# A SwiGLU down projection in seven products of halves, on a TensorE-bound kernel

## The chip, the cores and the metric

One core of one Trainium2 chip. The metric is the device time of one execution in microseconds (us). A core has these engines, each with its own queue, which it works through in the order of the program: TensorE (PE; loads of its stationary operand are shown as PEld), VectorE (DVE), ScalarE (ACT), GpSimd (POOL) and SyncE (SP), which here issues most of the DMAs. Matrix products go to PSUM, which PE writes and DVE and ACT read; everything else lies in SBUF.

## What is computed

A normalised input goes into two branches: attention over the last 512 positions of a cache (32 heads of 192), and a SwiGLU feed-forward network. The Silu of the second gates the first.

```
x  = A_x                                   # 2048 x 640
xn = layernorm(x)
s  = attention(xn, k_cache, v_cache, wq, wo)
h  = silu(xn @ w_gate) * (xn @ w_up)       # 2048 x 1536
g  = silu(h @ w_down)                      # w_down: 1536 x 640
out = x + s * g
```

The change concerns `h @ w_down` and the Silu around it.

## The kernel before

The kernel has three stages. The first, up to 171 us of the profiled execution, is the feed-forward network with the layer norm in front of it. The second, by far the longest, runs attention over 16 pairs of heads. The third is the output projection. Both attention's query projection and the output projection already use fewer products than a plain matrix product would: they add halves of operands first (`combine_wq`, `combine_x`, `a_sum`, `wo_sums`) and add halves of results later.

**The feed-forward stage.** The 2048 rows form four blocks of 512 (`b`), the 1536 hidden columns 12 groups of 128 (`f`). The loop from line 488 runs over `b` and, in it, over `f`. One step does:

- `ffn_hidden(b, f)` (line 377): ten products of 128x128 by 128x512 into a PSUM tile `sc` of two banks, five for the gate half, five for the up half; ACT takes the Silu of one half (line 374), and DVE multiplies it with the other into `hTs[b][:, f, :]` (line 375), which holds the hidden values transposed: 128 hidden columns on the partitions, 512 rows. There are two `sc` tiles in turn, so the products of step `f + 2` need the multiply of step `f`. Block 0 has its first four groups before the loop.
- `wo_sums` (line 346), in two of every three steps: DVE adds pieces of the output projection's weights, two sums in the first of the three steps, three in the second, into a tile `wo_s` that exists once; after the fifth sum SP stores it to `wo_d` (line 360), so the next group of sums, two steps on, waits until this store has landed. `wo_pieces` loads the pieces two groups ahead.
- in blocks 0 to 2, `ln_stats` (DVE, steps 2 to 5) and `ln_apply` with a DMA transpose (steps 6 and 7) for the next block's rows, whose loads SP issues at step 0.
- in blocks 2 and 3, one entry of `xwork` per step: a sum over blocks of `xn` (`combine_x`, DVE, 0.67 to 0.95 us each), which attention's query projection needs later. In the same blocks, the first pair's keys are loaded, transposed, summed and centred, and its query weights laid out.
- in blocks 1 to 3, at steps 1, 4, 7 and 10, `ffn_down(b - 1, u)` (line 383): one tile of 128 rows of the block before. For each of 12 hidden groups it runs two products of 128x128 by 128x320, into the two banks of one `mm` tile; then one ACT Silu over both halves (line 393) and one SP store of 128x640 to `g_d` (line 394).

After the loop (line 549) the last block's four `ffn_down` follow, with six `q_full` (line 396: five products of 128x512 and an ACT copy) between them, which project the first queries. There are two `mm` tiles in turn, used by `ffn_down`, `q_full` and, later, attention. Attention starts with `scores_phase(0, 0)`, in which `q_rows` writes `mm` tiles and `scores` writes `sc` tiles.

Buffers that attention uses later and that are empty in most of the feed-forward stage: `m_f` (32-bit sums of queries), the second buffer of each of `wq_p`, `khat` and `qT`.

All instructions stand in each engine's queue in the order in which the Python program issues them (`manual_schedule`); waits between engines are put in by the framework.

Of the kernel before, what the change touches and what calls it, by code (L numbers as in the profile page):

```python
# [9 lines left out]
ACT = mybir.ActivationFunctionType  # L10
ALU = mybir.AluOpType
# [4 lines left out]
def kernel(  # L16
# [13 lines left out]
    nc = tc.nc  # L30
    P = nc.NUM_PARTITIONS
# [3 lines left out]
    Sq, D = x2.shape  # L35
    _, Hkv, Sk, Dh = A_k_cache.shape
# [3 lines left out]
    W = min(4096, max(256, Sk // 4))  # L40
    assert Dh == 192 and W == 512 and Hkv == H and H % 2 == 0
    assert D % P == 0 and F % P == 0 and Sq % 512 == 0
    NC = D // P
    T = Sq // P
    NB = Sq // 512
    KC = W // P
    NF = F // P
# [4 lines left out]
    HC = D // 2  # L52
# [3 lines left out]
    bf = dt.bfloat16  # L56
    h16 = dt.float16
    f32 = dt.float32
# [10 lines left out]
    kpool = ctx.enter_context(tc.tile_pool(name="att_k", bufs=1))  # L69
    qpool = ctx.enter_context(tc.tile_pool(name="att_q", bufs=2))  # L70
# [3 lines left out]
    wpool = actx.enter_context(tc.tile_pool(name="att_w", bufs=2))  # L74
# [5 lines left out]
    def sc_tile():  # L80
        return sc_pool.tile([P, 2, 512], f32, name="sc")

    def mm_tile(which=None):
        which = mm_next[0] if which is None else which
        mm_next[0] = 1 - which
        return mm_pool[0].tile([P, 2, 512], f32, name="mm", tag="mm%d" % which)
# [8 lines left out]
    m_f = res.tile([P, 2, 2, 512], f32, name="m_f")  # L95

    o_d = dram.tile([T, P, 2 * KH, P], bf, name="o_d")
    g_d = dram.tile([T, P, D], bf, name="g_d")
# [110 lines left out]
    def q_of(i, j):  # L209
        return q_pair(i)[:, 3 * (i % 2) + j, :]  # L210
# [15 lines left out]
    with ExitStack() as fctx:  # L226
# [4 lines left out]
        ffa = fctx.enter_context(tc.tile_pool(name="ffa", bufs=3, side="right"))  # L231
# [5 lines left out]
        wd_sb = ffw.tile([P, NF, D], bf, name="wd_sb")  # L237
# [3 lines left out]
        def load_x(t, engs=(nc.sync,)):  # L241
            x_t[t] = lnx.tile([P, D], bf, name="x_t")
            n = P // len(engs)
            for k, eng in enumerate(engs):
                r = slice(k * n, (k + 1) * n)
                eng.dma_start(out=x_t[t][r, :], in_=x2[t * P + r.start : t * P + r.stop, :])
# [24 lines left out]
        for t in range(4, 8):  # L271
# [9 lines left out]
        first = [  # L281
            [gu[:, s, :] for s in range(2)]
            for gu in (sc_tile(), sc_tile(), psum1.tile([P, 2, 512], f32, name="gu"))
        ]
# [21 lines left out]
        def ln_rstd(b, t0, t1):  # L306

            mv, rstd = ln[b]
            nc.gpsimd.tensor_scalar(rstd[:, t0:t1], mv[:, t0:t1, 1], EPS, None, op0=ALU.add)
            nc.gpsimd.tensor_tensor(rstd[:, t0:t1], rstd[:, t0:t1], nhalf[:, t0:t1], ALU.pow)  # L310
# [24 lines left out]
        hTs, won = {}, {}  # L335
# [10 lines left out]
        def wo_sums(n, ks):  # L346

            t = won[n]
            if not ks.start:
                won["sums"] = ffw.tile([P, len(B_SUMS), 2, HC], h16, name="wo_s")  # L350
            sums = won["sums"]

            def piece(q):
                return t[:, q[0], :, q[1] * HC : (q[1] + 1) * HC]

            for k in ks:
                x, y, op = B_OF[B_SUMS[k]]
                nc.vector.tensor_tensor(sums[:, k, :, :], piece(x), piece(y), op)
            if ks.stop == len(B_SUMS):
                nc.sync.dma_start(  # L360
                    out=wo_d[:, :, 2 * n : 2 * n + 2, :].rearrange("s p c d -> p s c d"), in_=sums[:, :, :, :]
                )
# [9 lines left out]
        def hidden_gate(b, f, g, u):  # L372
            sg = ffa.tile([P, 512], bf, name="sg")
            nc.scalar.activation(sg[:], g, ACT.Silu)  # L374
            nc.vector.tensor_tensor(hTs[b][:, f, :], u, sg[:], ALU.mult)  # L375

        def ffn_hidden(b, f, gu=None):
            gu = gu or [sc[:, s, :] for sc in (sc_tile(),) for s in range(2)]
            for s in range(2):
                hidden_mm(gu[s], s, f, slice(b * 512, (b + 1) * 512))  # L380
            hidden_gate(b, f, *gu)

        def ffn_down(b, u):

            dn, rows = mm_tile(), slice(u * P, (u + 1) * P)
            for f in range(NF):
                for n in range(2):
                    nc.tensor.matmul(  # L388
                        dn[:, n, 0:HC], hTs[b][:, f, rows], wd_sb[:, f, n * HC : (n + 1) * HC],
                        start=(f == 0), stop=(f == NF - 1),  # L390
                    )
            g_t = ffa.tile([P, D], bf, name="g_t", bufs=2)
            nc.scalar.activation(g_t[:].rearrange("p (n d) -> p n d", n=2), dn[:, :, 0:HC], ACT.Silu)
            nc.sync.dma_start(out=g_d[4 * b + u, :, :], in_=g_t[:])

        def q_full(i, j):
            pr, b = divmod(i, NB)
            q_ps = mm_tile()[:, 0, :]
            for c in range(NC):
                nc.tensor.matmul(  # L400
                    q_ps[:, :], pairs[pr]["wq"][:, AS_IS[j], c, :], xnT[:, c, b * 512 : (b + 1) * 512],
                    start=(c == 0), stop=(c == NC - 1),
                )
            nc.scalar.copy(q_of(i, j), q_ps[:, :])
# [54 lines left out]
        for t in range(4):  # L459
            rows = slice(t * P, (t + 1) * P)  # L460
# [25 lines left out]
        xwork = []  # L486

        for b in range(NB):
            if b:
                hTs[b] = ffh.tile([P, NF, 512], bf, name="hT")  # L490
            nx = b + 1 < NB
            u = 0
            for f in range(NF):
                if nx and b and f == 0:
                    for t in range(4 * b + 4, 4 * b + 8):
                        load_x(t)
                if b or f >= 4:
                    ffn_hidden(b, f)
                n, phase = divmod((b - 1) * NF + f, 3)
                if n < KH // 2 and (b or n >= -2):  # L500
                    if b and phase < 2:
                        wo_sums(n, (range(0, 2), range(2, len(B_SUMS)))[phase])
                    if phase == 1 and n + 2 < KH // 2:
                        wo_pieces(n + 2)
                if nx and 2 <= f < 6:
                    ln_stats(4 * b + 2 + f)
                    if f == 5:
                        ln_rstd(b + 1, 0, 4)
                if nx and f in (6, 7):
                    for t in range(4 * b + 2 * f - 8, 4 * b + 2 * f - 6):  # L510
                        ln_apply(t)
                        ln_transpose_dma(t)
                if b == 2 and f == 0:
                    for half in range(2):
                        swap_x(DIFF[0], half, half)
                elif b == 2 and f == 8:
                    swap_x(DIAG, 0, 0)
                    xwork += x_combinations(DIFF[0]) + x_combinations(SUM[0])
                elif b == 3 and f == 0:
                    for half in range(2):  # L520
                        swap_x(DIFF[1], half, 2 + half)
                    swap_x(DIAG, 1, 3)
                elif b == 3 and f == 2:
                    xwork += [
                        u for to in (SUM[1], DIFF[1], DIAG) for u in x_combinations(to)
                    ]
                if xwork:
                    xwork.pop(0)()

                if b >= 1 and f in (1, 4, 7, 10):  # L530
                    ffn_down(b - 1, u)
                    u += 1
                if b == 2:
                    if f == 0:
                        load_k(0)
                    elif f == 3:
                        transpose_k(0)
                    elif f == 6:
                        load_wq(0)
                    elif 7 <= f < 10:  # L540
                        sum_k(0, f - 7)
                    elif f == 11:
                        combine_wq(0)
                elif b == 3:
                    if f < 5:
                        centre_k(0, f)
                    elif f < 7:
                        (load_k, load_wq)[f - 5](1)
        early_q = [(i, j) for i in range(2) for j in range(3)]
        for u in range(4):  # L550
            ffn_down(NB - 1, u)
            for _ in range((0, 2, 2, 2)[u]):
                q_full(*early_q.pop(0))
            if xwork:
                xwork.pop(0)()
        nc.scalar.activation(act_t[:], one_t[:], ACT.Exp)

# [247 lines left out]
    def store(n, side, cols=slice(0, D), eng=nc.sync):  # L805
        r = ROW_PAIRS[n][side]
        eng.dma_start(out=out2[r * P : (r + 1) * P, cols], in_=xg[n, side][:, 0, cols])

    V = nc.vector
# [8 lines left out]
    def total(to, x, y, op=ALU.add):  # L818
        V.tensor_tensor(to, x, y, op)
# [221 lines left out]
```

## Time and profile before

| what | value |
|---|---|
| median of three runs | 896.6 us (896.43 to 898.16) |
| the profiled execution | 898.59 us, span of its instructions 896.8 us |
| mean granted clock of TensorE | 0.996 |
| PE busy from 60 to 160 us, and from 160 to 180 us | 100.00 of 100 us, 19.54 of 20 us |
| `ffn_down`: products | 384 of 128x320, in 16 tiles, first 39.1 us, last 168.8 us |
| `ffn_down`: Silu | 16 of 128x640, mean 704 ns |
| `ffn_down`: stores | 16 of 160 KB, 1.8 to 6.2 us to landing, median 4.7 us |
| load of `w_down` | issued at 12.9 us, 12.7 us to landing |
| store of the wo sums | 12 of 800 KB, median 4.8 us to landing |

A time of an operation runs from its start to its end, and on DVE and PE the next one starts somewhat earlier than that end. Products on PE are pipelined: one of 320 columns has a length of 299 ns, but the next one starts long before. The chain of waits shows such a row of products with the time it holds PE. "Idle" at the end of a line is the time that the engine stood still in front of it, with what ended the wait.

### The profile page before, as it was taken

What the parts mean: (1) busy time and instruction counts of PE and PEld (TensorE: products, weight loads), DVE (VectorE), ACT (ScalarE), POOL (GpSimd) and SP (SyncE); (2) the same over time, 40 slices, a digit from 0 to 9 for tenths busy, and PEclk for the clock granted to TensorE, in tenths of its full rate; (3) what the DMA queues carried; (4) which work ended last, traced back from release to release, by engine and by line L of the source; (5) the groups of instructions that cost most, each with busy time, mean ns of one, the idle gap of its engine ahead of it and who ended that gap; (6) DMA issues with size and microseconds to landing.
All of it is one profiled execution on the core that took longest, in us unless ns stands there. A gap on an engine that the chain in (4) does not pass through costs nothing.

```text
span 896.8 us, 22912 instructions
## 1 busy us (share of the span) xinstructions
PE 879.9 (98%) x9705; PEld 582.5 (65%) x9705; DVE 599.0 (67%) x1020; ACT 404.2 (45%) x577; POOL 114.2 (13%) x215
## 2 busy tenths in 40 slices
PE   9999999999999999999999999999999989999997
PEld 6455555567667666667667666666676756777775
DVE  6464775276776776877777776777775367666664
ACT  4222222565765765765765765766757200000000
POOL 0000001012222222122212222222200000000000
PEclk9999999999999999999999999999999999999999
DMA  9669876256986979886986976978889997655520
GB/s 300 168 190 260 225 221 198 60 99 155 238 180 147 175 193 199 167 170 150 241 176 149 171 184 122 212 177 171 177 205 234 253 342 247 204 182 173 177 72 15
DMA packets 270822, 165.50 MB, mean 185 GB/s; under 512 B 173952, under 2 KB 265984, under 8 KB 270080
## 3 DMA queue, kind: packets, MB, share of 16 engines
q1 hardware_dynamic: 262896, 149.99, 69.9%
q10 hardware_dynamic: 7824, 14.06, 4.6%
q8 instruction: 76, 1.25, 0.6%
q14 instruction: 26, 0.21, 0.1%
HBM read 88.18 MB, written 40.24 MB: 143 GB/s over the span
## 4 chain that ended last, share of the span: by engine, by line
PE 90%; DMA 6%; DVE 2%; SPq 1%; issue 1%; ACTq 0%; ACT 0%
PE sc L645 18%; PE acc L780 15%; PE mm L591 12%; PE sc L367 11%; PE mm L684 10%; PE sc L684 9%; PE mm L577 8%; PE mm L388 6%; DMA b_w<-in_A_wo_dram 3%; DMA V_p<-in_A_v_cache_dram 2%; PE mm L400 1%; SPq L716 1%; DVE a_s L773 1%; DMA x_t<-in_A_x_dram 1%; PE gu L367 0%
## 5 line engine op out<-in xcount | busy, mean ns | idle before, releaser
L649 ACT ACTIVATE p_t<-sc 128x1024 bf16<-128x1024 f32 x256 | 253.7, 1024 | 60.0 <-PE sc L645 55.5
L645 PE MATMUL sc<-qT,khat 64*128 64x512 bf16 x1536 | 198.0, 376 | 0.0
L684 PEld LDWEIGHTS <-p_t 64*128 64x128 bf16 x4096 | 172.9, 94 | 14.3 <-DMA V_p<-in_A_v_cache_dram 4.1
L645 PEld LDWEIGHTS <-khat 64*128 64x128 bf16 x1536 | 89.0, 94 | 75.1 <-issue 0.3
L780 PEld LDWEIGHTS <-a_s 128*128 128x128 f16 x960 | 95.1, 99 | 44.4 <-DVE a_s L773 3.4
L684 PE MATMUL mm<-V_p,p_t 64*128 64x193 bf16 x2112 | 112.3, 243 | 4.5 <-DMA V_p<-in_A_v_cache_dram 4.4
L780 PE MATMUL acc<-b_w,a_s 128*128 128x320 f16 (+1 forms) x768 | 110.6, 305 | 5.3 <-DVE a_s L773 2.6
L684 PE MATMUL sc<-V_p,p_t 64*128 64x193 bf16 x1984 | 104.8, 243 | 0.0
L582 DVE TENSOR_REDUCE qT<-mm 128x512 bf16<-128x1024 f32 x66 | 80.6, 1222 | 29.7 <-PE mm L577 27.3
L591 PE MATMUL mm<-xc,wq_p 64*128 64x512 f16 x750 | 94.4, 376 | 0.0
L591 PEld LDWEIGHTS <-wq_p 64*128 64x128 f16 (+1 forms) x1050 | 58.7, 94 | 47.6
L629 POOL TENSOR_TENSOR m_f<-m_f 128x1024 f32<-128x1024 f32 x28 | 65.8, 2350 | 178.0 <-DVE qT L624 178.0
L713 ACT ACTIVATE O_b<-sc,r 128x192 bf16<-128x192 f32 x124 | 45.5, 420 | 92.4 <-PE sc L684 83.6
L577 PE MATMUL mm<-xnT,wq_p 64*128 64x512 bf16 x660 | 82.9, 376 | 0.5 <-DVE qT L582 0.5
L773 DVE TENSOR_TENSOR a_s<-a_q 128x3072 f16<-128x3072 bf16 x40 | 69.4, 1750 | 12.6 <-DMA a_q<-o_d 6.3
L375 DVE TENSOR_TENSOR hT<-sc,sg 128x512 bf16<-128x512 f32 x46 | 31.5, 687 | 44.3 <-ACT sg L374 44.2
L367 PE MATMUL sc<-xnT,wg_sb 128*128 128x512 bf16 (+1 forms) x260 | 60.2, 354 | 0.6 <-issue 0.5
L367 PE MATMUL sc<-xnT,wu_sb 128*128 128x512 bf16 (+1 forms) x260 | 60.3, 354 | 0.0
L577 PEld LDWEIGHTS <-wq_p 64*128 64x128 bf16 x660 | 36.2, 94 | 36.8 <-issue 5.7
L702 DVE RECIPROCAL r<-mm 128x4 f32<-128x4 f32 x66 | 12.0, 182 | 71.0 <-PE mm L684 70.9
L374 ACT ACTIVATE sg<-sc 128x512 bf16<-128x512 f32 x46 | 27.3, 596 | 69.1 <-PE sc L367 66.0
L624 DVE TENSOR_TENSOR qT<-mm,m_f 128x1024 bf16<-128x1024 f32 x30 | 36.7, 1224 | 31.3 <-ACT m_f L621 31.3
(78 smaller groups left out, 859.1 us busy)
## 6 DMA issues: line engine op xcount, KB each, us to landing
o_d<-OT_b SPq DMA_DIRECT2D x64, 384.0 KB, 5.9
a_q<-o_d SPq DMA_DIRECT2D x28, 768.0 KB, 6.3
wo_d<-wo_s SPq DMA_DIRECT2D x12, 800.0 KB, 4.8
won<-in_A_wo_dram SPq DMA_DIRECT2D x24, 320.0 KB, 5.4
wq_rows<-in_A_wq_dram SPq DMA_DIRECT2D x16, 480.0 KB, 4.8
b_w<-wo_d ACTq DMA_DIRECT2D x4, 1920.0 KB, 10.2
wq_rows<-in_A_wq_dram SPq DMA_DIRECT2D x30, 240.0 KB, 5.9
K_p<-in_A_k_cache_dram SPq DMA_DIRECT2D x32, 192.0 KB, 6.4
```

The source lines that it names most:

```text
L367: nc.tensor.matmul(out, w_sb[:, c, f * P : (f + 1) * P], xnT[:, c, qc], start=(c == 0), stop=(c == NC - 1),)
L388: nc.tensor.matmul(dn[:, n, 0:HC], hTs[b][:, f, rows], wd_sb[:, f, n * HC : (n + 1) * HC], start=(f == 0), stop=(f == NF - 1),)
L577: nc.tensor.matmul(q_ps[:, h, :], w[r, AS_IS[j], c, :], xnT[r, c, b * 512 : (b + 1) * 512], start=(c == 0), stop=(c == NC - 1),)
L582: nc.vector.reduce_sum(q_of(i, j), q_ps[:, :, :].rearrange("p h n -> p n h"), axis=AX.X)
L591: nc.tensor.matmul(ps[:, h, :], ws[h][r, c, :], xs[h][r, c, :], start=(first and c == 0), stop=(c == NC - 1), skip_group_check=True,)
L629: eng.tensor_tensor(m_f[:, SIDE_S, :, :], diag, m_f[:, SIDE_S, :, :], ALU.subtract)
L645: nc.tensor.matmul(sc[:, h, :], khat[r, j, ks], q_of(i, j)[r, :], start=(j == 0), stop=(j == 2))
L649: nc.scalar.activation(p_t[:, :, :], sc[:, :, :], ACT.Exp, scale=scale)
L684: m = nc.tensor.matmul(acc[:, k, h * 256 : h * 256 + Dh + 1], Ps[i][kc][r, h, qt * P : (qt + 1) * P], V_p[r, kc, h, 0 : Dh + 1], start=(p ...
L713: nc.scalar.activation(O_b[:, qt, h, :], a_k[:, h, 0:Dh], ACT.Copy, scale=r[:, k, h, :])
L773: nc.vector.tensor_tensor(a_s[n, m][:], a_q[n, x][:], a_q[n, y][:], op)
L780: nc.tensor.matmul(ps[k] if ns > 1 else ps, at[:, c, :], b_w[m][:, c, k * w : (k + 1) * w], start=(first and c == 0), stop=(c == KH - 1), ...
```

## The change

`ffn_down` now takes two row tiles at a time, `u` and `u + 2` of a block. It cuts the contraction of 1536 into two halves of six groups (index `k`) and the 640 columns into two halves of 320 (`n`), and computes the two by two blocks of the result by seven products of halves, W1 to W7, instead of eight. Each product is six matmuls of 128x128 by 128x320.

- **Sums of the weights**, once, by DVE, in block 0 at steps 8 to 11 (`wd_sum`): T1, T2, T3, T4, each 6 x 320 elements per partition in half precision. T3 takes the place of one quarter of `w_down`, the others lie in `m_f` and in a `wq_p` buffer.
- **Sums of x** per pair of row tiles, by DVE: S1 to S4, each 6 x 128 elements, from `hTs`, in half precision, in the buffers of `wq_p`, `khat` and `qT`.
- **Three accumulators** in the two `mm` tiles: U and V are the two banks of the first, W is a bank of the second. U is used by W1, then W6 and W7 and W4 add to it; V by W2; W by W5, then W3 adds to it. Between those, ACT copies out U after W1 (`p1`) and after W6 (`u2`), and W after W5 (`w5`), in 32 bits, and DVE adds V to `p1`, U to `w5`, W to `u2` in 32 bits (`total`).
- **Four gates** per pair, each an ACT Silu over 128x320: of `p1`, `w5`, `u2` and, out of PSUM, U. Two stores per pair, one after W3 and one after W4.
- **Places**: in blocks 1 to 3, one product per step after the hidden products, two at steps 5 and 11, so that a pair takes six steps. After the loop, the last block's 14 products follow one another, with a `q_full` after numbers 0, 3, 6, 8, 10 and 13.
- **`q_full`** writes an `sc` tile in place of an `mm` tile.
- **`xwork`**: in block 3 one entry in every second step in place of every step; six entries are left for the stretch behind the loop, one after each of the products 1 to 6.

```diff
         def ffn_hidden(b, f, gu=None):
...
+        KD = NF // 2
+        W1, W2, W6, W5, W7, W3, W4 = range(7)
+
+        room = [
+            m_f[:, :, :, :].rearrange("p a b n -> p (a b n)").bitcast(h16),
+            wpool.tile([P, 5, NC, P], bf, name="wq_p")[:, :, :, :].rearrange("p a c n -> p (a c n)").bitcast(h16),
+            kpool.tile([P, 3, W], bf, name="khat", bufs=2)[:, :, :].rearrange("p a n -> p (a n)").bitcast(h16),
+            qpool.tile([P, 6, 512], bf, name="qT")[:, :, :].rearrange("p a n -> p (a n)").bitcast(h16),
+        ]
...
+        T1, T4, T2 = (carve(k, KD * HC).rearrange("p (c d) -> p c d", d=HC) for k in (0, 0, 1))
+        T3 = quarter(0, 1).bitcast(h16)
+        S1, S2, S3, S4 = (carve(k, KD * P).rearrange("p (c q) -> p c q", q=P) for k in (1, 2, 2, 3))
+        p1, u2, w5 = (carve(3, 2 * HC).bitcast(f32) for _ in range(3))
+        D_OF = {W1: quarter(0, 0), W2: quarter(1, 0), W6: T2, W5: T1, W7: T3, W3: quarter(1, 1), W4: T4}
+
+        def wd_sum(n):
+
+            to, x, y = (
+                (T1, quarter(0, 1), quarter(0, 0)), (T2, quarter(1, 1), T1),
+                (T3, quarter(1, 1), quarter(0, 1)), (T4, quarter(1, 0), T2),
+            )[n]
+            nc.vector.tensor_tensor(to, x, y, ALU.subtract)
+
         def ffn_down(b, u):
 
-            dn, rows = mm_tile(), slice(u * P, (u + 1) * P)
-            for f in range(NF):
-                for n in range(2):
+            st = {}
+
+            def a(side, k):
+                rows = slice((u + 2 * side) * P, (u + 2 * side + 1) * P)
+                return hTs[b][:, k * KD : (k + 1) * KD, rows]
+
+            def mm(m, at, ps, first=True):
+                for c in range(KD):
                     nc.tensor.matmul(
-                        dn[:, n, 0:HC], hTs[b][:, f, rows], wd_sb[:, f, n * HC : (n + 1) * HC],
-                        start=(f == 0), stop=(f == NF - 1),
+                        ps, at[:, c, :], D_OF[m][:, c, :],
+                        start=(first and c == 0), stop=(c == KD - 1), skip_group_check=True,
                     )
-            g_t = ffa.tile([P, D], bf, name="g_t", bufs=2)
-            nc.scalar.activation(g_t[:].rearrange("p (n d) -> p n d", n=2), dn[:, :, 0:HC], ACT.Silu)
-            nc.sync.dma_start(out=g_d[4 * b + u, :, :], in_=g_t[:])
+
+            def total(to, x, y, op=ALU.add):
+                nc.vector.tensor_tensor(to, x, y, op)
+
+            def gate(side, n, x):
+                nc.scalar.activation(st["g"][side][:, n * HC : (n + 1) * HC], x, ACT.Silu)
+
+            def store(side):
+                nc.sync.dma_start(out=g_d[4 * b + u + 2 * side, :, :], in_=st["g"][side][:])
+
+            def w1():
+                ps = [mm_tile() for _ in range(2)]
+                st["U"], st["V"], st["W"] = ps[0][:, 0, 0:HC], ps[0][:, 1, 0:HC], ps[1][:, 0, 0:HC]
+                st["g"] = [ffa.tile([P, D], bf, name="g_t", bufs=2) for _ in range(2)]
+                mm(W1, a(0, 0), st["U"])
+                nc.scalar.copy(p1, st["U"])
+                total(S1, a(1, 0), a(1, 1))
+                total(S2, S1, a(0, 0), ALU.subtract)
+
+            def w2():
+                mm(W2, a(0, 1), st["V"])
+                total(p1, st["V"], p1)
+                gate(0, 0, p1)
+
+            def w6():
+                mm(W6, S2, st["U"], False)
+                nc.scalar.copy(u2, st["U"])
+                total(S3, a(0, 0), a(1, 0), ALU.subtract)
+
+            def w5_():
+                mm(W5, S1, st["W"])
+                nc.scalar.copy(w5, st["W"])
+                total(S4, a(0, 1), S2, ALU.subtract)
+
+            def w7():
+                mm(W7, S3, st["U"], False)
+                total(w5, st["U"], w5)
+                gate(1, 1, w5)
+
+            def w3():
+                mm(W3, S4, st["W"], False)
+                total(u2, st["W"], u2)
+                gate(0, 1, u2)
+                store(0)
+
+            def w4():
+                mm(W4, a(1, 1), st["U"], False)
+                gate(1, 0, st["U"])
+                store(1)
+
+            return [w1, w2, w6, w5_, w7, w3, w4]
 
         def q_full(i, j):
             pr, b = divmod(i, NB)
-            q_ps = mm_tile()[:, 0, :]
+            q_ps = sc_tile()[:, 0, :]
...
-                if xwork:
+                if xwork and (b == 2 or f % 2 == 0):
                     xwork.pop(0)()
 
-                if b >= 1 and f in (1, 4, 7, 10):
-                    ffn_down(b - 1, u)
-                    u += 1
+                if b == 0 and f >= 8:
+                    wd_sum(f - 8)
+                elif b and f == 0:
+                    downs = ffn_down(b - 1, 0) + ffn_down(b - 1, 1)
+                for _ in range((2 if f in (5, 11) else 1) if b else 0):
+                    downs.pop(0)()
...
         early_q = [(i, j) for i in range(2) for j in range(3)]
-        for u in range(4):
-            ffn_down(NB - 1, u)
-            for _ in range((0, 2, 2, 2)[u]):
+        for n, do in enumerate(ffn_down(NB - 1, 0) + ffn_down(NB - 1, 1)):
+            do()
+            if n in (0, 3, 6, 8, 10, 13):
                 q_full(*early_q.pop(0))
-            if xwork:
+            if xwork and n:
                 xwork.pop(0)()
```

Within one step the program issues, in this order: the hidden products with their Silu and multiply, the wo sums, the layer norm's work, the entry of `xwork`, the down products with their copies, totals and gates, and last the work for the first pair of heads.

More of the change, by code (lines that the diff above doesn't have):

```diff
@@ new lines, in carve, with quarter @@
+        def carve(k, n):
+            part, room[k] = room[k][:, 0:n], room[k][:, n:]
+            return part
+        def quarter(k, n):
+            return wd_sb[:, k * KD : (k + 1) * KD, n * HC : (n + 1) * HC]
+        T1, T4, T2 = (carve(k, KD * HC).rearrange("p (c d) -> p c d", d=HC) for k in (0, 0, 1))
+        T3 = quarter(0, 1).bitcast(h16)
+        S1, S2, S3, S4 = (carve(k, KD * P).rearrange("p (c q) -> p c q", q=P) for k in (1, 2, 2, 3))
+        p1, u2, w5 = (carve(3, 2 * HC).bitcast(f32) for _ in range(3))
@@ L491 @@
             nx = b + 1 < NB
-            u = 0
             for f in range(NF):
```

## The prediction

> **What bounds the kernel now.** I read the page first, then the chain of waits up to 240 us, then the timelines of DVE, ACT and PE over the feed-forward stage, which ends at 171 us.
>
> ```profile
> PE 879.9 (98%) x9705; PEld 582.5 (65%) x9705; DVE 599.0 (67%) x1020; ACT 404.2 (45%) x577; POOL 114.2 (13%) x215
> ```
> ```profile
> 136.61 3.26 PE mm L388 x24
> 139.87 6.47 PE sc L367 x30
> 146.34 3.26 PE mm L388 x24
> 149.60 2.16 PE sc L367 x10
> 151.76 6.52 PE mm L388 x48
> 158.28 2.16 PE mm L400 x10
> ```
>
> PE is the bound. In the stage the chain is PE alone: three hidden steps (one `f` is 6.47/3 = 2.157 us), a down tile (3.26 us), without a gap. One 128x320 product takes 3.26/24 = 0.136 us. The stretch from 60 to 100 us, first PE, then PEld and DVE:
>
> ```profile
> 60.00:100.00 40.00, 40.00 (x226) 21.89 (x225) 22.59 (x52) 9.98 (x16) 1.27 (x2) 1.00 0.92 237
> ```
>
> DVE has 17 of 40 us free, ACT 30; the clock is full and DMA is at 0.92. The durations I use (name, shapes, count, then busy and mean ns):
>
> ```profile
> L375 DVE TENSOR_TENSOR hT<-sc,sg 128x512 bf16<-128x512 f32 x46 | 31.5, 687 | 44.3 <-ACT sg L374 44.2
> L374 ACT ACTIVATE sg<-sc 128x512 bf16<-128x512 f32 x46 | 27.3, 596 | 69.1 <-PE sc L367 66.0 <-DVE xn L325 1.6 <-DVE wo_s L358 1.6
> L358 DVE TENSOR_TENSOR wo_s<-won 128x640 f16<-128x640 bf16 x60 | 26.1, 482 | 5.2 <-DMA wo_d<-wo_s 4.0 <-DMA won<-in_A_wo_dram 1.1
> L393 ACT ACTIVATE g_t<-mm 128x640 bf16<-128x640 f32 x16 | 11.3, 704 | 42.7 <-PE mm L388 42.7
> ```
>
> And the timelines (start, length): DVE at a full step (`f` = 4), twice where it waits for the store of the wo sums, and two neighbours of ACT and PE.
>
> ```profile
> 49.95 0.63 DVE L375 TENSOR_TENSOR hT<-sc,sg 128x512 bf16<-128x512 f32 x1
> 50.50 1.28 DVE L358 TENSOR_TENSOR wo_s<-won 128x640 f16<-128x640 bf16 x3
> 51.71 0.88 DVE L301 BATCH_NORM_STATS2 stats<-x_t 128x6 f32<-128x320 bf16 x2
> 52.62 0.21 DVE L304 BATCH_NORM_AGGREGATE mv<-stats 128x2 f32<-128x12 f32 x1
> ...
> 88.61 0.89 DVE L358 TENSOR_TENSOR wo_s<-won 128x640 f16<-128x640 bf16 x2 [1.48 <-DMA wo_d<-wo_s]
> ...
> 108.09 0.89 DVE L358 TENSOR_TENSOR wo_s<-won 128x640 f16<-128x640 bf16 x2 [1.49 <-DMA wo_d<-wo_s]
> ```
> ```profile
> 151.80 0.60 ACT L374 ACTIVATE sg<-sc 128x512 bf16<-128x512 f32 x1 [1.45 <-PE sc L367]
> ```
> ```profile
> 150.52 1.24 PE L367 MATMUL sc<-xnT,wu_sb 128*128 128x512 bf16 x5
> ```
>
> The last two say two things. ACT starts 0.04 us after the end of the products it needs (150.52 + 1.24 = 151.76), and it waited for the `u` half of the tile, although it reads the `g` half: a wait on a PSUM tile is for the whole tile here.
>
> **The change part by part.** *Products.* A pair of row tiles costs 42 products in place of 48. Eight pairs: 48 x 0.136 = **-6.5 us**, all on the bound. Half-precision operands cost PE nothing: the 64x512 products take 376 ns both at L577 (bf16) and L591 (f16).
>
> *Sums of the weights.* Four of 1920 elements in block 0, steps 8 to 11. From L358 (640 in 482 ns) and L773 (3072 in 1750 ns) a 16-bit sum costs 0.52 ns an element over 0.15 us: 1.15 us each. A step there has 1.47 us of idle DVE (before 30.68 us in its timeline). Nothing, and 1.15 us each without that idle time.
>
> *New work per pair.* DVE: four sums of x, 768 elements, 0.55 us by the same line, 0.47 from start to start; three totals of 320 from PSUM, 0.49 us by L375 and L707 (384 in 554 ns), 0.41 from start to start. ACT: three copies and four gates of 320, 0.43 each (L393 and L374: 0.84 ns an element over 0.16), for two gates of 0.70 before. By amount it fits: 8 x 0.47 + 6 x 0.41 = 6.2 us of DVE in a block of 37.
>
> *New waits.* Order decides, for each queue runs in program order. The totals stand at the end of DVE's step, behind its multiply (0.61 from start to start), wo sums (0.80 for two, 1.21 for three) and statistics (1.04). A gate waits for its total, and the next step's Silu stands behind that gate on ACT, the next multiply behind the Silu. And the products reuse three accumulators, so W4 waits for `w5`'s total, and the next pair's W1 for the last gate. I walk block 1 from the end of the hidden products of `f` = 4 (time 0), with 0.16 us for a product to drain, 0.04 for a signal, 0.08 for DVE's last write:
> - DVE: multiply 0.83 to 1.44, wo sums to 2.65, statistics to 3.69, W7's total to 4.10. ACT: gate 4.22 to 4.65, Silu of `f` = 5 only then, to 5.25 (without the gate: from 3.17).
> - PE: W7 to 0.82, hidden 5 to 2.97, W3 to 3.79, W4 when the total is read: 4.22, **0.4 late**.
> - DVE: multiply 5.28 to 5.89, statistics 6.93, W3's total 7.34. ACT: two gates, to 8.32. PE: W4 to 5.04, hidden 6 to 7.19, W1 of the second pair at 8.36, **1.2 late**.
> - The Silu of `f` = 6 is thus late too; multiply, wo sums, two normalisations, S1, S2 end at 12.05, W2's total at 15.14. W6 follows hidden 8 at 14.3, but writes in the tile of that total: **1.0 late**. The first pair's W6 loses 0.2 likewise.
>
> Block 1: 0.2 + 0.4 + 1.2 + 1.0 = 2.8. Block 2 has the same queues, and in its second pair the centring sums and sums of x before W7's total: 0.4 more, 3.2. Block 3 has no statistics, but starts on block 2's late gates (W1 1.1) and has 1.3 in five small waits: 2.4. **Behind block 3** no hidden products lie between W4 and the next W1: from the end of hidden 10, multiply, wo sums, a sum of x (0.87) and total end at 3.93, gate 4.5, Silu 5.1, multiply 5.75, total 6.16, two gates 7.18; W4 is over at 4.87, W1 starts at 7.2: 2.35 late. Then W6 waits for a total (0.2 + 0.41 + 0.12 = 0.7), the second W2 for a copy (0.7), the second W1 0.2: 4.0. Sum: 2.8 + 3.2 + 2.4 + 4.0 = **+12.4**. The queries that follow products there (six of 1.08 us) cover the rest; `sc_tile` for them costs nothing, since their copies (0.59) end within the next product.
>
> *The store of the wo sums.* Its one buffer is needed again two steps later. Before, a down tile lay between steps 1 and 3 and between 7 and 9: 2 x 2.157 + 3.26 = 7.6 us; now 2 x (2.157 + 0.815) = 5.9. From the end of the third sum to the next use that leaves 4.7. The store took 88.61 - 80.75 = 7.9 in block 2 at step 1 and 108.09 - 100.31 = 7.8 at step 7 (SP was still issuing K loads and transposes), 4.7 to 6.3 elsewhere. DVE would stand still 3.2 at the first: S4 is then late for W3 by 0.8, W7's total for W4 by 2.4 in place of 0.4: +2.8. At step 7, 3.1 by the old landing; SP's transposes have more of a lead over the sums now, so I take 1.3 at W4. Block 3's 1.1 to 1.6 go into slack. **+4.1**; bounds 0 (all land in 4.7) and 5.8 (old landings, block 3 with 0.9).
>
> *SP and moved steps.* Two stores of `g_t` stand at steps 5 and 11 in place of one at 1, 4, 7, 10; those of step 11 hold SP until the last gate, ahead of four loads of x (2.07 us of issue, 6.6 to landing). The statistics that need them come two steps and 8 us later: nothing, or below 1 us. The sums of x that move behind block 3 run while PE has 17.9 us of products; the last W1 pays its 0.2 above. Other tile buffers swap places; bounds -0.5 and +0.5, taken 0.
>
> **Two prices only rows near by bound.** S2 and S4 mix bf16 and f16 inputs, which no row has. Lower bound 0.47 (all 16-bit inputs), upper 0.87 at L375's 1.05 ns an element: the walk then loses 3.3 more. I take 0.47, as the f16 result of bf16 inputs at L358 runs at that pace.
>
> The Trainium skill, page "VectorE: DVE Perf Modes", section "What auto-detection actually checks", asks for tensors of 16 bits and step 1, not for one type; L358 agrees with that, and by it the dearer case falls away.
>
> The second is the wait for a whole PSUM tile. If writes waited only for readers of their own bank, W6 and the second W2 would lose nothing (4.6 us), some of which returns at W4, and the +12.4 would be 8.4. Against it stands the Silu that waited for the other half.
>
> The Trainium skill, page "PSUM — Partial Sum Buffer", section "PSUM bank collisions raise a hardware error", says that engines on different banks don't disturb each other and asks for a guard by bank. By that rule the sum would be -6.5 + 8.4 + 4.1 = +6.0; the Silu of this trace waits longer than the rule needs.
>
> **Sum.** -6.5 + 12.4 + 4.1 = **+10.0**. The profiled execution took 898.6 us (span 896.8) against a median of 896.6, a difference that the sum doesn't touch: 896.6 + 10.0 = **906.6 us**.
>
> **The rivals.** *(a) The slack holds and most of the saving lands.* The point is step 4: if DVE reached W7's total 1.3 us sooner than my 4.10 (by shorter small operations, or a Silu not held by the gate), W4, the next W1 and W6 would find their accumulators free; only the 2.35 behind block 3 would stay: 896.6 - 6.5 + 2.4 = 892.5. For it: DVE's 17 idle us in 40. Against: the idle time lies in other steps than 3, 4, 6, 7.
> *(b) Waits by bank and stores that land in 4.7:* -6.5 + 8.4 = +1.9, 898.5. For it: most stores landed so. Against: the two of 7.8.
> *(c) DVE dearer or stores later still:* mixed sums at 0.87, old landings: -6.5 + 12.4 + 5.8 + 3.3 = +15.0, 911.6. For it: DMA at 0.92 and a walk with no slack left, so each late sum goes straight to PE.
>
> **How the numbers follow.** Forecast 0.60 (its own range 901 to 910), (a) 0.14, (b) 0.13, (c) 0.13. A measurement of this kernel tells about 0.2% (1.8 us) from no change. Faster: (a) and a little of (b), 0.15. Within: 0.05 of (b). Slower: the rest, 0.80. Range: up to (c) whole, 912, and down to (b), 898; only (a) is outside.
>
> **What would show it.** PE waits of about 1 to 2.5 us in front of W1 and W4, released by ACT gates and DVE totals; the Silu of `f` = 5 some 1.5 us behind its products; the stage ending near 181 us in place of 171; DVE waiting for `wo_d` at steps 3 of block 2 by 2 us or more. Wrong would be: PE whole through the stage and its end near 165 us (a); W6 never released by DVE (waits by bank).

## The result, and the profile after

The changed kernel takes 910.2 us (median of 6 runs, 904.2 to 914.4) beside 896.6 us before (6 runs, 893.1 to 898.2): 1.0148 times as long, interval 1.0118 to 1.0178. The profiled execution is at the upper end: 914.4 us, span 912.6.

Busy time by engine of the changed kernel, then the chain of work that ended last, by engine, before and after:

```profile
PE 880.2 (96%) x9641; PEld 579.3 (63%) x9657; DVE 629.0 (69%) x1080; ACT 415.6 (46%) x617; POOL 113.6 (12%) x215
```
```profile
PE 90%; DMA 6%; DVE 2%; SPq 1%; issue 1%; ACTq 0%; ACT 0%
PE 80%; DMA 8%; DVE 7%; SPq 2%; issue 1%; ACT 1%; ACTq 0%; DVEq 0%
```

PE works as long as before (880.2 us for 879.9) with 48 products less, as the counts of weight loads show (9657 for 9705; a few records of products are missing). Part of the products ran at half clock, and the chain that was all PE in this stage now runs through DVE too. The feed-forward stage ends at 183.5 us in place of 171.2, which is 12.3 of the 15.8 us between the two spans. The stretch of block 2, before and after (start to end, its length, then PE, PEld, DVE, ACT, POOL, the clock and DMA):

```profile
73.70:112.66 38.96, 38.96 (x218) 21.14 (x217) 25.32 (x54) 9.98 (x16) 1.27 (x2) 1.00 0.95 246
```
```profile
74.81:119.98 45.17, 39.60 (x202) 20.28 (x204) 31.42 (x68) 12.62 (x26) 1.27 (x2) 0.96 0.88 227
```

The block has fewer products, takes 6 us longer, and the mean clock is 0.96. PE in the first pair of this block: W7, the products of step 5's up half, and what follows (start, length, idle time in front):

```profile
89.13 0.98 PE L424 MATMUL mm<-wd_sb,khat 128*128 128x320 f16 x6
...
91.02 1.24 PE L367 MATMUL sc<-xnT,wu_sb 128*128 128x512 bf16 x5
93.07 0.99 PE L424 MATMUL mm<-wd_sb,qT 128*128 128x320 bf16 x6 [0.80 <-DVE qT L430]
96.26 0.97 PE L424 MATMUL mm<-m_f,hT 128*128 128x320 f16 x6 [2.21 <-DVE qT L430]
97.07 2.25 PE L367 MATMUL sc<-xnT,wg_sb 128*128 128x512 bf16 x5
99.12 1.96 PE L367 MATMUL sc<-xnT,wu_sb 128*128 128x512 bf16 x5
100.92 0.98 PE L424 MATMUL mm<-wd_sb,hT 128*128 128x320 bf16 x6
```

W3 (93.07) waits for S4, W4 (96.26) for W7's total. Then ten products of 512 columns take 3.85 us, from 97.07 to 100.92, where they take 2.16 elsewhere. The granted clock was at half there (rows in the last section). DVE shows the causes of the two waits, the late store in front of step 3's wo sums and the order at step 4:

```profile
87.05 0.69 DVE L375 TENSOR_TENSOR hT<-sc,sg 128x512 bf16<-128x512 f32 x1 [0.69 <-ACT sg L374]
90.66 0.89 DVE L358 TENSOR_TENSOR wo_s<-won 128x640 f16<-128x640 bf16 x2 [2.92 <-DMA wo_d<-wo_s]
91.47 0.88 DVE L301 BATCH_NORM_STATS2 stats<-x_t 128x6 f32<-128x320 bf16 x2
92.38 0.21 DVE L304 BATCH_NORM_AGGREGATE mv<-stats 128x2 f32<-128x12 f32 x1
92.51 0.50 DVE L430 TENSOR_TENSOR qT<-hT,khat 128x768 f16<-128x768 bf16 x1
92.93 0.68 DVE L375 TENSOR_TENSOR hT<-sc,sg 128x512 bf16<-128x512 f32 x1
93.53 1.29 DVE L358 TENSOR_TENSOR wo_s<-won 128x640 f16<-128x640 bf16 x3
94.73 0.88 DVE L301 BATCH_NORM_STATS2 stats<-x_t 128x6 f32<-128x320 bf16 x2
95.65 0.21 DVE L304 BATCH_NORM_AGGREGATE mv<-stats 128x2 f32<-128x12 f32 x1
95.77 0.44 DVE L430 TENSOR_TENSOR qT<-mm,qT 128x320 f32<-128x320 f32 x1
```

The total at 95.77 is what W4 waits for; W7's products had been done since 90.1. The store that held DVE up to 90.66 belongs to sums that ended at 82.72; SP issued it at 83.62, behind two loads of K, and it took 6.9 us to landing. The coupling through ACT is seen without the late store, in block 1, steps 4 and 5:

```profile
49.45 0.60 ACT L374 ACTIVATE sg<-sc 128x512 bf16<-128x512 f32 x1 [1.79 <-PE sc L367]
53.40 0.47 ACT L433 ACTIVATE g_t<-qT 128x320 bf16<-128x320 f32 x1 [3.35 <-DVE qT L430]
53.77 0.58 ACT L374 ACTIVATE sg<-sc 128x512 bf16<-128x512 f32 x1
```

The hidden products of step 5 ended at 52.3; their Silu starts at 53.77, behind a gate that stood 3.35 us for DVE. PE's waits in this block, at W4 and at the second pair's W1 and W6:

```profile
53.42 0.97 PE L424 MATMUL mm<-m_f,hT 128*128 128x320 f16 x6 [0.28 <-DVE qT L430]
57.35 0.97 PE L424 MATMUL mm<-wd_sb,hT 128*128 128x320 bf16 x6 [0.80 <-ACT g_t L433]
64.27 0.97 PE L424 MATMUL mm<-wq_p,khat 128*128 128x320 f16 x6 [0.81 <-DVE qT L430]
```

**Where the time of the stage went.** I took each start of a row of products less the end of PE's issue in front of it (start plus products times 0.136 or 0.216 us). Block 1 lost 2.6 us in waits, block 2 6.2, block 3 2.8, the stretch behind it 3.9: 15.5 us. Two stretches at half clock took 1.7 (97.07 to 100.92) and 1.6 us (162.23 to 165.68) more. -6.5 + 15.5 + 3.3 = 12.3. The other 3.5 us of the two profiled spans lie behind the stage: attention, from its first query rows to the first output product, took 531.5 us against 529.1, the rest 197.6 against 196.5. Nothing points to the change: in the eight experiments below, with the same code from there on, attention took 523.6 to 531.2 us and the rest 195.3 to 198.2.

### The profile page after: what moved, and what is told of

Same layout as the page of the kernel before. It is cut to its first block, busy times and chain, and to the rows that moved or that the text cites. A ratio compares the mean times of both kernels' runs of the same rounds, so it can differ in the third digit from the quotient of the medians.

```text
span 912.6 us, 22901 instructions
## 1 busy us (share of the span) xinstructions
PE 880.2 (96%) x9641; PEld 579.3 (63%) x9657; DVE 629.0 (69%) x1080; ACT 415.6 (46%) x617; POOL 113.6 (12%) x215
## 4 chain that ended last, share of the span: by engine, by line
PE 80%; DMA 8%; DVE 7%; SPq 2%; issue 1%; ACT 1%; ACTq 0%; DVEq 0%
PE sc L731 17%; PE acc L866 15%; PE mm L677 12%; PE mm L770 10%; PE sc L770 9%; PE mm L663 7%; PE sc L367 6%; DMA b_w<-in_A_wo_dram 3%; PE mm L424 3%; DMA V_p<-in_A_v_cache_dram 2%; DVE wo_s L358 2%; DMA wo_d<-wo_s 1%; DVE hT L375 1%; PE sc L484 1%; DVE qT L430 1%
## 5 line engine op out<-in xcount | busy, mean ns | idle before, releaser
L866 PE MATMUL acc<-b_w,a_q 128*128 128x320 f16 x384 | 54.6, 299 | 0.0
```

What stands on the lines that cost most here:

```text
L866: nc.tensor.matmul(ps[k] if ns > 1 else ps, at[:, c, :], b_w[m][:, c, k * w : (k + 1) * w], start=(first and c == 0), stop=(c == KH - 1), ...
```

## The experiments

Each kernel is the changed one with the edit shown, timed beside the kernel before (896.6 us in both groups).

**The products alone.** The edit leaves out the sums of x, the copies and the totals; after W4 one gate reads both banks of the first tile and two read the second tile.

```diff
                 mm(W1, a(0, 0), st["U"])
-                nc.scalar.copy(p1, st["U"])
-                total(S1, a(1, 0), a(1, 1))
-                total(S2, S1, a(0, 0), ALU.subtract)
...
-                mm(W6, S2, st["U"], False)
-                nc.scalar.copy(u2, st["U"])
-                total(S3, a(0, 0), a(1, 0), ALU.subtract)
+                mm(W6, a(1, 0), st["U"], False)
```

> The 42 products per pair alone, on the row tiles as they are: the sums of x, the copies and the totals are left out, and the gates read PSUM after W4 (so the output is not the reference's). If the loss lies in the waits of the queues (theory A), PE gets its 6.5 us back and pays about 1 us where W1 follows W4 directly behind block 3: about 891 us, with no PE wait over 0.3 us inside blocks 1 to 3. If the products themselves cost PE more than 0.136 us each, by mixed types or by adding to an accumulator again (theory B), it stays above 896 us and the row of six products is longer than 0.82 us.

Measured: 893.2 us, ratio 0.9963 (0.9948 to 0.9977). A row of six products holds PE for 0.81 us as before, so theory B is out. Theory A's bound on waits was missed at two places: 0.94 us for a transposed x at the start of block 1, and this one, PE and DVE:

```profile
112.12 1.24 PE L367 MATMUL sc<-xnT,wg_sb 128*128 128x512 bf16 x5 [1.74 <-DVE hT L375]
```
```profile
109.00 0.89 DVE L358 TENSOR_TENSOR wo_s<-won 128x640 f16<-128x640 bf16 x2 [4.45 <-issue]
```

With no sum or total in it, DVE stood 4.45 us in front of the wo sums of step 9 in block 2: the store before them was issued at 102.80 us and took 6.1 to landing. So the new place of the products alone brings the next use of `wo_s` too near to its store, which SP issued 1.9 us behind the end of its sums (100.86). The first hidden product of block 3 paid 1.7 us behind it (the last transposed x landed then as well, at about 111.9 us, so the price is not DVE's alone).

**V in the second tile.**

```diff
-                st["U"], st["V"], st["W"] = ps[0][:, 0, 0:HC], ps[0][:, 1, 0:HC], ps[1][:, 0, 0:HC]
+                st["U"], st["V"], st["W"] = ps[0][:, 0, 0:HC], ps[1][:, 1, 0:HC], ps[1][:, 0, 0:HC]
```

> Only V moves, into the free bank of the second tile. If a wait holds for a whole PSUM tile (theory A), W6 no longer waits for the total of V, nor the second W2 behind the loop for the copy of U: their waits of the changed kernel (0.2 to 1.0 us, some 4 us in all) are gone, of which 1.5 come back at W4: about 907.5 us. If writes wait only for readers of their own bank (rival), nothing changes: 910 us and the same waits at W6.

Measured: 905.9 us, ratio 1.0082 (1.0052 to 1.0111). The second pair's W6 of block 1, which started 0.98 us late (64.27 us, 0.81 of it idle), follows the hidden products at once:

```profile
61.73 1.24 PE L367 MATMUL sc<-xnT,wu_sb 128*128 128x512 bf16 x5
62.81 0.98 PE L424 MATMUL mm<-wq_p,khat 128*128 128x320 f16 x6
```

None of the waits in front of W6 is left, nor that of the second W2 behind the loop. U and V lay in different banks before, so the wait was for the tile. Part of the gain returns elsewhere: in this profile W4 of block 2's second pair stood 2.54 us in place of 1.24.

**The down products' work first in each step.**

```diff
                 if b or f >= 4:
                     ffn_hidden(b, f)
+                if b == 0 and f >= 8:
+                    wd_sum(f - 8)
+                elif b and f == 0:
+                    downs = ffn_down(b - 1, 0) + ffn_down(b - 1, 1)
+                for _ in range((2 if f in (5, 11) else 1) if b else 0):
+                    downs.pop(0)()
                 n, phase = divmod((b - 1) * NF + f, 3)
```

> Each step's down products, sums and totals are issued right behind the hidden products, ahead of the wo sums, statistics and normalisations; the amount of work is the same. Theory A (order on DVE and ACT): W7's total ends some 2.2 us sooner in its step, gates no longer hold the Silu, waits fall from 15.5 to about 9 us, two of them in block 2 for the store of the wo sums, and the drops of the clock behind the longest waits go in part: 899 to 902 us. Rival (DVE has too much to do in total): 908 to 912 us, with the waits moved to the hidden products.

Measured: 899.4 us, ratio 1.0018 (1.0001 to 1.0034). The same instructions in another order give back 11 of 13.6 us. DVE at step 4 of block 1:

```profile
49.51 0.69 DVE L375 TENSOR_TENSOR hT<-sc,sg 128x512 bf16<-128x512 f32 x1
50.12 0.48 DVE L430 TENSOR_TENSOR qT<-mm,qT 128x320 f32<-128x320 f32 x1
50.52 1.29 DVE L358 TENSOR_TENSOR wo_s<-won 128x640 f16<-128x640 bf16 x3
```

The total stands right behind the multiply now, where it stood behind the statistics (at 52.93 us in the changed kernel), and no wait is left in block 1. Block 2 keeps 1.6 and 1.3 us at W4, where the store is late, and no product ran at half clock.

**Two tiles and two stores for the wo sums.**

```diff
-            if not ks.start:
-                won["sums"] = ffw.tile([P, len(B_SUMS), 2, HC], h16, name="wo_s")
-            sums = won["sums"]
+            sums = ffw.tile([P, len(ks), 2, HC], h16, name="wo_s", tag="wo_s%d" % min(ks.start, 1))
...
-            if ks.stop == len(B_SUMS):
-                nc.sync.dma_start(
-                    out=wo_d[:, :, 2 * n : 2 * n + 2, :].rearrange("s p c d -> p s c d"), in_=sums[:, :, :, :]
-                )
+            nc.sync.dma_start(
+                out=wo_d[ks.start : ks.stop, :, 2 * n : 2 * n + 2, :].rearrange("s p c d -> p s c d"),
+                in_=sums[:, :, :, :],
+            )
```

> The wo sums get two tiles, one for the first two and one for the other three, each with a store of its own, so that a tile is needed again three steps after its store and not two; as many bytes, 12 DMA issues more. If the wait for the store is what W3 and W4 pay in block 2 (theory A), DVE's waits of up to 2.9 us and PE's waits of 0.8, 2.2 and 1.2 us at W3 and W4 shrink to about 0.4 each, and the drop of the clock behind the 2.2 us goes: 902 to 905 us. If it is the DMA bandwidth of the stage (rival), the wait moves to other users: 908 us or more.

Measured: 900.8 us, ratio 1.0054 (1.0034 to 1.0074), better than expected. All that DVE waits for in the stage, and block 2's two W4:

```profile
DVE hT L373 <- ACT sg L372: 28.4, 30, 2.4
DVE qT L428 <- PE mm L422: 7.4, 5, 3.2
```
```profile
92.64 0.97 PE L422 MATMUL mm<-m_f,hT 128*128 128x320 f16 x6 [0.28 <-DVE qT L428]
113.87 0.97 PE L422 MATMUL mm<-m_f,hT 128*128 128x320 f16 x6 [0.48 <-DVE qT L428]
```

DVE waits for no store any more, block 2's W4 waits 0.28 and 0.48 us in place of 2.21 and 1.24, and the clock is full throughout the stage. As many bytes are stored, so what cost time was the landing of a store just ahead of the next use of its tile, not the amount stored. The edit does two things about it, and the run doesn't separate them: it puts the next use one step later, and the smaller stores land sooner (median 2.4 and 3.2 us in place of 4.6).

**Both of the last two.**

> The two edits that each took back most of the loss, together: the down products' DVE and ACT work right behind the hidden products, and two tiles with two stores for the wo sums. Theory A (the two causes are the order on DVE and the late store, and nothing else of size): no PE wait is left in blocks 1 to 3; behind them the first W1 1.4 us, W6 0.7, the second W1 and W2 0.9 together. Stage end 171.2 - 6.5 + 3.0 = 167.7 us, time about 893 us. Rival (both edits took back the same wait): like the better one alone, 899 us.

Measured: 893.6 us, ratio 0.9968 (0.9955 to 0.9982). PE's waits over the whole stage:

```profile
PE mm L422 <- ACT g_t L431: 1.2, 1, 1.2
PE sc L365 <- DVE wd_sb L410: 0.8, 1, 0.8
PE mm L422 <- DVE qT L428: 0.7, 1, 0.7
PE mm L422 <- ACT qT L441: 0.6, 1, 0.6
```

Three of them lie behind the loop, as expected. The one of 0.8 us is the first hidden product of block 1, at 35.41 us. The view puts it down to a sum of the weights, which ended at 34.91 us and which this product doesn't read; the last transposed x of the block, which it does read, was issued at 31.9 us and took 3.4, so it landed at 35.3. The kernel before stands 0.45 us at the same place.

**The gate of U ahead of the other.**

```diff
                 total(u2, st["W"], u2)
-                gate(0, 1, u2)
-                store(0)
...
                 gate(1, 0, st["U"])
                 store(1)
+                gate(0, 1, u2)
+                store(0)
```

> In W4 the gate of U, which frees the accumulator, is issued ahead of the gate that waits for W3's total. Theory A: the waits of W1 for the last gate (0.8 and 0.9 us in blocks 1 to 3 and 2.0 us behind them) fall by 0.5 to 0.9 each, some 3 us in all, of which W6 takes back 1: 907 to 908 us. Rival (U is free late because of PE or of the Silu in front, not because of the order of the two gates): no change, 910 us.

Measured: 905.6 us, ratio 1.0099 (1.0075 to 1.0124), some 2 us better than expected. The first W1 behind the loop, in the changed kernel and in this one:

```profile
162.23 1.76 PE L424 MATMUL mm<-wd_sb,hT 128*128 128x320 bf16 x6 [1.96 <-ACT g_t L433]
```
```profile
159.50 0.97 PE L424 MATMUL mm<-wd_sb,hT 128*128 128x320 bf16 x6 [0.53 <-ACT g_t L433]
```

Its idle time falls from 1.96 to 0.53 us, no product at half clock follows it, and no other W1 waits. W6 takes some of it back: 1.22 us in block 1 in place of 0.81, 0.98 in block 3 in place of 0.23.

**The sums of x back.**

```diff
-                if xwork and (b == 2 or f % 2 == 0):
+                if xwork:
```

> Only the other part of the change is undone: in block 3 a sum of x again in every step, none is left for the stretch behind the loop. Theory A (DVE has no slack in block 3): W6 and W1 there wait some 0.9 us longer each, the first W1 behind the loop 0.9 more: 3 us more than the changed kernel, about 913 us. Rival (the moved sums cost more behind the loop than they did in it): 907 to 909 us.

Measured: 912.2 us, ratio 1.0170 (1.0148 to 1.0193). The first W1 behind the loop waits 3.07 us, where it waited 1.96; W6 in block 3 waits 1.1 and 1.2, where it waited 0.23 and 0.46. The intervals of this kernel and of the changed one overlap, so the 2 us between them are not shown by the times; the waits in the profiles are.

**All four edits, and one query projection ahead of the first W1 behind the loop.**

```diff
         for n, do in enumerate(ffn_down(NB - 1, 0) + ffn_down(NB - 1, 1)):
+            if n == 0:
+                q_full(*early_q.pop(0))
             do()
-            if n in (0, 3, 6, 8, 10, 13):
+            if n in (3, 6, 8, 10, 13):
```

> All four edits that take a wait away (work of the down products first on DVE and ACT, two tiles for the wo sums, V in the second tile, the gate of U first) and the first query projection moved ahead of the first W1 behind the loop. Theory A: nothing of the named waits is left, the stage ends 6.5 us earlier than before the change, at 164.7 us, and the time is 890 to 891 us, below the kernel before. Rival (something not named, such as DMA, keeps a part): 893 us or more, with PE waits in the stage.

Measured: 891.0 us, ratio 0.9940 (0.9920 to 0.9961), faster than the kernel before. The stage ends at 166.8 us, 2.1 later than expected:

```profile
PE sc L365 <- ACT g_t L431: 1.4, 1, 1.4
PE sc L365 <- DMA xnT<-xn: 0.9, 1, 0.9
PE mm L663 <- DVE qT L668: 0.3, 1, 0.3
```

The last is in attention and was there before. The other two are the first hidden product of block 1 and of block 3. The view puts the first down to a gate, which ended at 111.11 us, just before the product's start at 111.16; but the last transposed x of block 3 was issued at 105.9 us and took 5.2, so it landed at 111.1 as well, and a hidden product reads x, not a gate. PE now comes to a block early enough to wait for the layer norm's transposes: the rival, in a small part.

## Why the prediction was right, point by point

- **Sign and cause**: as forecast, the products saved 6.5 us and the queues took more. The edits that only change an order, a tile or a store bring the time under that of the kernel before (893.6 us with order and stores alone), with the same work on DVE and ACT, so the amount of this work doesn't explain the loss.
- **The walk of block 1** is borne out to 0.1 us at three of its four waits: 0.2, 0.4, 1.2 and 1.0 were forecast at W6, W4, the second W1 and the second W6; 0.20, 0.45, 0.96 and 0.98 were measured.
- **The new waits without the late store** (12.4 us) **and the store** (4.1): 16.5 forecast, 15.5 measured. Block 2 took 6.2 for 7.3 (3.2 + 4.1): its second W1 found U free, as the hidden products in front of it ran at half clock (with V apart and with the sums of x back, where the clock stayed full there, this W1 stood 0.79 us); W4 of the second pair lost 1.4 for 1.7. Of these 1.7, 1.3 had been booked to the store of step 7. In the profile it landed at about 113.1 us, and the pieces of the weights for step 9, which the view names for DVE's 0.66 us there, some 0.1 us later, so that share isn't shown to be the store's. Block 3 took 2.8 for 2.4, the stretch behind it 3.9 for 4.0. DVE stood 2.9 us in front of the sums of step 3, for 3.2.
- **A term that the sum lacked**: products at half clock behind waits of 2 us. In the profiled execution, the slowest of the six, they cost 3.3 us. The median, 13.6 above the kernel before, lies beyond the forecast's 10.0 and beyond its own range (901 to 910) by a little. The mean clock was 0.987 to 0.992 in five of the six executions and 0.995 in the fastest (904.2 us); the kernel before had 0.993 to 0.997 in its 41 executions beside the experiments. This fits falls of the clock in most executions, but how much of the 3.6 us they make up in the median is not shown, as only one was profiled.
- **The price of mixed sums**: S2 of f16 and bf16 took 557 ns, S1 of two bf16 operands 550. I had taken the cheaper bound, and it holds. The Trainium skill, page "VectorE: DVE Perf Modes", section "What auto-detection actually checks", asks for 16-bit tensors and not for one type, and these rows agree.
- **The wait for a whole PSUM tile**: taken, and shown by the kernel with V apart. The Trainium skill, page "PSUM — Partial Sum Buffer", section "PSUM bank collisions raise a hardware error", asks for a guard by bank, which is less than these waits do; the sum by it, +6.0, was too low.
- **Edits costed at nothing**: the sums of the weights took 1.15 us each, as forecast, and PE did not wait for them. The loads of x held nothing up: at step 2 of block 2 DVE runs the statistics straight behind its multiply (84.81 us).
- **The rivals.** (a), the saving whole, was off by the order at steps 3 to 7, as its own condition said: with the totals earlier and two stores, it is nearly reached (893.6 us; 899.4 with the totals earlier alone). (b) needed waits by bank and stores in time; neither held. (c) names a time nearer the measured one, 911.6, but by luck: mixed sums were not dearer, and DVE stood 2.9 us for the late store, not more than the 3.2 forecast.

## What to carry to other kernels

Before an algebraic saving on the bound engine, write down for each accumulator that is used again what must be read first, and where this read stands in its engine's queue: here an operation of 0.4 us at the end of DVE's step made ACT stand 3.35 us, and the next Silu with it. Put what frees an accumulator, and what another engine's queue stands behind, ahead of work that nobody waits for. Moving products within a loop also moves the distance between a store and the next use of its buffer; count it anew.

## What the runs showed of the chip that I had not expected

The clock falls after waits of 2 us, and not always. The changed kernel in four stretches of 1 us each (start to end, length, PE, PEld, DVE, ACT, POOL, then the clock):

```profile
96.00:97.00 1.00, 0.74 (x6) 0.55 (x6) 0.21 (x1) 0.76 (x2) 0.00 (x0) 1.00 1.03 351
97.00:98.00 1.00, 1.00 (x5) 0.44 (x4) 0.77 (x2) 0.20 (x1) 0.00 (x0) 0.58 0.98 218
98.00:99.00 1.00, 1.00 (x4) 0.30 (x2) 0.96 (x4) 0.00 (x0) 0.00 (x0) 0.50 0.93 209
...
101.00:102.00 1.00, 1.00 (x8) 0.65 (x8) 0.19 (x1) 0.66 (x2) 0.00 (x0) 1.00 0.64 222
```

After 2.21 us of idle PE at 94 to 96 us, the clock is at half from 97 for some 3.4 us, which cost 1.7. An idle time of 2.20 us at the same W4 was followed by half clock with the gate of U first, but by none with V apart or with the sums of x back; one of 1.96 us in front of the first W1 behind the loop was in the changed kernel, but not with V apart or with two stores. Those of 2.54 (V apart) and 3.07 us (the sums of x back) were; behind the last the clock was at half for some 6.8 us, from 162.9 to 169.7. No shorter wait of these profiles was, between 34 and 190 us. So a wait of about 2 us costs either itself or itself and 1.6 us more; what decides between the two is not shown. Runs of one kernel may differ by that: those of the changed kernel lie 10 us apart, those before 5. The Trainium skill, page "TensorE: Matmul & The Clock Gate", section "What's actually happening", describes a free-running window of 3.4 us, which fits the length at half clock and the chance in it; its section "HAM oscillation — how this bites in real kernels" puts the rule as no idle gaps above 3.4 us, and here gaps of 2.0 to 2.5 us were enough.
